# An attention and mixture-of-experts kernel: two addends move from TensorE to VectorE, one matmul group moves within a round, one product moves from GpSimd to VectorE

## The chip, the cores and the metric

One core of a Trainium2 chip runs the whole kernel in one launch. The metric is the device time of the launch in microseconds; the number to predict is the median over several runs. The engines are called by their names in the profile: PE (TensorE matmuls), PEld (its weight loads), DVE (VectorE), ACT (ScalarE), POOL (GpSimd) and SP (SyncE, here the queue that issues most transfers).

## What is computed

```python
# attention: 4 batches, 8 heads, 768 steps, head size 48
for t in range(S):
    cur   = einsum('bhd,bhe->bhde', u * k[t], v[t])
    y[t]  = einsum('bhd,bhde->bhe', r[t], state + cur)
    state = w * state + einsum('bhd,bhe->bhde', k[t], v[t])
# then, on x = y as 3072 tokens of 384 numbers:
P = exp(x @ w_gate - max);  8 rounds of: rows to sum 1, columns to sum 1, times N/E
out = sum over 8 experts of P[:, e] * (relu(x @ w1[e]) @ w2[e])     # hidden size 1024
```

All numbers are float32; the inputs and the result are in device memory.

## The kernel before, in words

The work has two stages. The attention stage (the first 207 us or so) treats the 3072 tokens as 24 tiles of 128; six tiles make one sequence, so the state starts anew at tiles 0, 6, 12 and 18. Beside it PE already computes a good part of expert 0. The expert stage (the rest) computes the other experts with a scheme of fewer products and writes the result.

The attention stage is one Python loop over rounds, `for i in range(NTT + 3)`, with i = 0 the first round; i = 11 is the twelfth. Every engine call goes through a wrapper that keeps the order in which the program was written, so **each engine executes its instructions in the order in which the loop emits them**; engines wait for each other by semaphores only. All such instructions have the wrapper's line, L30, in the profile, and are told apart by their tiles.

In round i, on PE, from i = 11 on:

- `stage_b(i+1)` transposes r and k of the next tile (`prT`, `pkT`, into PSUM); ACT copies them out as `rT` and `kT`;
- `stage_c(i)` makes the scores of tile i (`pA`, two PSUM banks, 64x64 pieces of PE); DVE copies them under the causal mask into `at`;
- `work(1)` executes one unit of expert 0: either 9 matmuls (`ph`) or 12 matmuls (`po`) of 384 columns, whose result ACT (and for `ph` DVE too) takes out;
- `state_part(i-1)` multiplies rT of the tile before with the state `S` (`py<-S,rT`, 64x64 pieces); `scores_part(i-1)` adds the product of `at` with v (`py<-vn,at`, 128x32 pieces); `state_product(i)` makes the state's increase (`py<-vn,kp`, 128x32 pieces);
- two or three more units of expert 0.

Before i = 11 the unit between `stage_c` and `state_part` is absent.

On ACT, the order around these is: the results of the units of the last round, now and then a half-precision copy of token sums (`xv<-ws`), the scaling of x (`xsc<-x,xs`, which needs DVE's `xs`), then `rT`, then `kT`. On DVE: the mask copies, a unit's low part (`hb<-ph,hb`), `x<-py,rk`, `S<-py,S`, the largest magnitude of x and its power of two (`xm` to `xs`), token sums, `kp`, the low part of x.

PSUM tiles of the tag `pa` share four buffers in turn. From i = 6 on, a round takes six: prT, pkT, pA for even and odd heads, and two for y (`y_banks`, called by `state_part` or `scores_part`, whichever comes first). So y's two banks are the buffers of that round's prT and pkT.

For the first four tiles (`tt < NE`) PE adds two addends to y by a product with the identity matrix (`addends`): the tile's `xadd` (in `hbx`, zeros in the normal case) and the bonus term `av` (in `rk`); ACT then copies y into x. From tile 4 on POOL adds `xadd` to the bonus term, and DVE adds that to y as it takes y out (`sum_x`).

`state_sum` makes the next state: DVE adds the old one (`S<-py,S`), POOL multiplies it with the decay `wbd` (`S<-S,wbd`). At the start of a sequence and for the first tiles DVE makes the product itself.

Of the kernel before, what the change touches and what calls it, by code (L numbers as in the profile page):

```python
# [13 lines left out]
ALU = mybir.AluOpType  # L14
# [19 lines left out]
def rwkv_sinkhorn_moe(  # L34
# [13 lines left out]
    V, S_, G, T, Q = (  # L48
        InOrder(tc, e) for e in (nc.vector, nc.scalar, nc.gpsimd, nc.tensor, nc.sync)
    )  # L50

    B, H, S, D = r.shape
# [6 lines left out]
    NTT = NT // P  # L59
# [10 lines left out]
    FHC = FH // P  # L70
    NPR = 15
    NE = 4

    const = ctx.enter_context(tc.tile_pool(name="const", bufs=1))
    sm = ctx.enter_context(tc.tile_pool(name="sm", bufs=2))
# [13 lines left out]
    def part(home, dtype, at, shape):  # L89

        n = 1
        for s_ in shape:
            n *= s_
        x_ = home if home.dtype == dtype else home.bitcast(dtype)
        x_ = x_[:, at : at + n]
        if len(shape) == 1:
            return x_
        names = "abcd"[: len(shape)]
        return x_.rearrange(
            f"p ({' '.join(names)}) -> p {' '.join(names)}", **{c_: s_ for c_, s_ in zip(names[1:], shape[1:])}  # L100
        )
# [14 lines left out]
    def xadd(t):  # L116
        return part(hbx, F32, t * DM, (DM,))
# [171 lines left out]
    def whole(gen):  # L289
        for _ in gen:  # L290
            pass
# [103 lines left out]
    wbd = ac.tile([P, NPAIR, D], F32, name="wbd")  # L395
# [134 lines left out]
    def prep(tt):  # L530
        ld_ = loads[tt]
        st[tt] = {}
        G.tensor_tensor(rp_[tt % 2][:, :, :D], ld_["r"], rt4, op=ALU.mult)
        if 0 < tt - 2 < NE:
            bonus(tt - 2)
        (G if 2 <= tt <= 2 * NE else V).tensor_tensor(kp_[tt % 3][:, :, :D], ld_["k"], kt4, op=ALU.mult)
        if tt == 2:
# [11 lines left out]
    def bonus(tt):  # L549
        vn = loads[tt]["v"]  # L550
        dg = at2.tile([P, H], F32, tag="dg", name=f"dg_{tt}")
        V.tensor_reduce(dg, st[tt]["rk"], axis=AX.X, op=ALU.add)
        av = st[tt].pop("rk")
        G.tensor_tensor(av, vn, dg.unsqueeze(2).broadcast_to([P, H, D]), op=ALU.mult)
        if tt >= NE:
            aq = av.rearrange("p h d -> p (h d)")
            G.tensor_tensor(aq, aq, xadd(tt), op=ALU.add)
        st[tt]["av"] = av

    def stage_b(tt):  # L560
        d = st[tt]
        for nm, src in (("rT", rp_[tt % 2]), ("kT", kp_[tt % 3])):
            pool, tag = (ps2, "po") if tt <= NE + 1 else (ps3, "pa")
            pt = pool.tile([P, NPAIR, P], F32, tag=tag, name=f"p{nm}_{tt}")
# [25 lines left out]
    def state_product(tt):  # L590
# [3 lines left out]
        kp = kp_[tt % 3].rearrange("p (a j) d -> p a (j d)", j=2)  # L594
        carry = 0 < tt < NE
        if tt:
# [11 lines left out]
    def state_sum(tt):  # L608
        d = st[tt]
        if "du" not in d:  # L610
            return
        pu = d["du"]
        sn = ss_[tt % 3]
        if tt < NE or tt % NCHB == 0:
            V.tensor_tensor(sn, pu, wbd, op=ALU.mult)
        else:
            V.tensor_tensor(sn, pu, d["S"], op=ALU.add)
            G.tensor_tensor(sn, sn, wbd, op=ALU.mult)
        st[tt + 1]["S"] = sn

    def y_banks(tt):
# [5 lines left out]
    def addends(tt):  # L627
        d = st[tt]
        d["py"] = y_banks(tt)
        for n, x_ in enumerate((xadd(tt).rearrange("p (h d) -> p h d", d=D), d["av"])):  # L630
            xg = x_.rearrange("p (a g) d -> p g a d", g=2)
            for g in range(2):
                T.matmul(d["py"][g], ident, xg[:, g], start=(n == 0), stop=False, skip_group_check=True)
        if tt + 1 < NE:
            T.matmul(d["pu"], ident, st[tt + 1]["S"], start=False, stop=False, skip_group_check=True)

    def state_part(tt):
        d = st[tt]
        if tt % NCHB == 0:
            return  # L640
        fresh = "py" not in d
        if fresh:
            d["py"] = y_banks(tt)
        for p_ in range(NPAIR):
            for g in range(2):
                rows = slice(g * HP, (g + 1) * HP)
                for hs in (slice(0, HP), slice(HP, C)):
                    T.matmul(
                        d["py"][g][hs, p_, :], d["rT"][rows, p_, hs], d["S"][rows, p_, :],
                        start=(fresh and p_ == 0), stop=False, skip_group_check=True,  # L650
                    )

    def scores_part(tt):
        d = st[tt]
        vn = loads[tt]["v"]
        at = at_[tt % 2]
        fresh = "py" not in d
        if fresh:
            d["py"] = y_banks(tt)
        for h in range(H):  # L660
            for q in range(0, P, QP):
                T.matmul(
                    d["py"][h % 2][q : q + QP, h // 2, :], at[:, h, q : q + QP], vn[:, h, :],
                    start=(fresh and h < 2), stop=(h >= H - 2), skip_group_check=True,
                )

    def sum_x(tt):
        d = st[tt]
        x = at2.tile([P, DM], F32, tag="x", name=f"x_{tt}")
        xv = x.rearrange("p (a g d) -> p g a d", g=2, d=D)  # L670
        if tt < NE:
            for g in range(2):
                S_.copy(xv[:, g], d["py"][g])
            d["x"] = x
            return
        av = d["av"].rearrange("p (a g) d -> p g a d", g=2)
        for g in range(2):
            V.tensor_tensor(xv[:, g], d["py"][g], av[:, g], op=ALU.add)
        d["x"] = x
# [148 lines left out]
    def work(n, hold=False):  # L828
        held[0] = hold
        for _ in range(n):  # L830
            if units:
                whole(units.pop(0))
        held[0] = False
# [15 lines left out]
    def run(i, place):  # L849
        for f in hooks.pop((i, place), []):  # L850
            f()
# [52 lines left out]
    for i in range(NTT + 3):  # L904
        if 1 <= i <= NE:
            stage_b(i + 1)
        run(i, "turned")
        if i + 2 < NTT and i != TH + 1:
            prep(i + 2)
        if i > NE:  # L910
            send_x(i)
        leave(0)
        if i + 1 < NTT:
            bonus_dot(i + 1)
        if NE < i < NTT - 1:
            stage_b(i + 1)
        if 1 <= i <= NE:
            addends(i - 1)
        if i <= NE:
            send_x(i)  # L920
        n = i + 5 if i < 2 else i + 4
        if i != 2 and n < NTT:
            load_part(n, "r", r)
            load_part(n, "k", k)
        if i == 0:
            load_part(3, "v", v)
        if i == 8:
            Q.dma_start(wg, w_gate.rearrange("(c p) e -> p c e", p=P))
        run(i, "loads")
        if NE <= i < NTT:  # L930
            bonus(i)
        leave(1)
        run(i, "early")
        if i < NTT:
            stage_c(i)
        if i > 10:
            work(1)
        run(i, "masked")
        if 1 <= i <= NTT:
            state_part(i - 1)  # L940
            scores_part(i - 1)
        if 2 <= i <= TH + 1:
            turn_x(i - 2)
        if i < NTT:
            state_product(i)
        if 1 <= i <= NTT:
            sum_x(i - 1)
        if i < NTT:
            state_sum(i)
        if 1 <= i <= NTT:  # L950
            bound_x(i - 1)
        if i > NTT:
            work(2)
        run(i, "middle")
        if 2 <= i < NTT - 2:
            load_part(i + 2, "v", v)
        for _ in range(n_steps(i)[0]):
            prepare()
        if i <= NTT:
            if i > TH:  # L960
                work(1 if i == 4 else 3 if i == 10 else 2, hold=i < 10)
            elif i == 0:
                S_.copy(onesb, ones)
                S_.copy(ident16, ident)
        run(i, "end")
        for _ in range(n_steps(i)[1]):
            prepare()
        if i == TH:
            prep(i + 3)
            scale_x(TH - 1)  # L970
            run(i, "last")
            units += [g1_unit(0, fc, 0) for fc in range(FHC)]
            units += [g2_half(0, t, 0, 0) for t in range(TH)]
        done = i - 2
        if TH <= done < NTT and done % TH == TH - 1:
            po_ = done // TH
            for p_, j in ((1, 0), (0, 1), (1, 1)) if po_ == 1 else ((po_, 0), (po_, 1)):
                turn[0] += 1
                g1 = [g1_unit(p_, fc, turn[0]) for fc in range(j * FHC, (j + 1) * FHC)]
                units += merged(g1, [g2_half(*a_) for a_ in pend])  # L980
                pend = [(p_, t, j, turn[0]) for t in range(TH)]
# [402 lines left out]
    for s in range(NS):  # L1384
        tasks = stage_tasks(s)
        for g in range(NG):
            for j in range(2):
                for n, nxt in enumerate(g1_slots(s, g, j)):
# [3 lines left out]
                    i = j * NPR + n  # L1392
# [37 lines left out]
```

## Time and profile before

| | |
|---|---|
| median of 3 runs | 1514.29 us (1514.22 to 1514.66) |
| the profiled execution, its own time | 1514.62 us |
| its span in the profile | 1513.1 us |
| busy: PE, DVE, ACT, POOL | 1501.1, 1010.1, 674.8, 586.8 us |
| granted PE clock | full in all slices of the span |

The span begins with the first instruction and ends with the last one; the execution's own time also holds what lies around it, 1.5 us. PE has work in 99% of the span.

### The profile page before, as it was taken

The page shows a single profiled execution, that of the slowest core. Times are in us where ns is not written, and L with a number is a line of the kernel's source. Part 1 is how long each engine was busy: PE and PEld are TensorE (multiplying, and loading weights), DVE is VectorE, ACT ScalarE, POOL GpSimd, SP SyncE. Part 2 cuts the span into 40 slices and gives each one's busy share as a digit, 9 for nine tenths or more (in the row PEclk, how much of TensorE's full clock was granted, in tenths as well). Part 3 has the DMA queues.
Part 4 walks back from the last instruction along what each step waited for, and adds up shares of the span by engine and source line. Part 5 has one row for each costly group of instructions (what it writes and reads, how often), then busy time and mean ns, then how long its engine had stood idle before and what let it go on. Part 6 is the DMA issues. An engine that isn't in the chain of part 4 may idle for free.

```text
span 1513.1 us, 28843 instructions
## 1 busy us (share of the span) xinstructions
PE 1501.1 (99%) x11654; PEld 846.7 (56%) x11656; DVE 1010.1 (67%) x1678; ACT 674.8 (45%) x1206; POOL 586.8 (39%) x687
## 2 busy tenths in 40 slices
PE   9999999999999999999999999999999999999999
PEld 7767766555555555555555555555555555555555
DVE  7998859676666666666676666666565666566464
ACT  6534425345354544445454544445353544444320
POOL 8878966200224243342425243242424233242200
PEclk9999999999999999999999999999999999999999
DMA  8965532212255576657666666655554454555434
GB/s 164 163 115 119 113 89 78 79 46 75 81 106 62 83 130 93 123 80 128 90 88 114 91 127 92 116 61 99 61 94 56 60 99 59 97 61 96 58 95 130
DMA packets 184840, 142.69 MB, mean 94 GB/s; under 512 B 107137, under 2 KB 178562, under 8 KB 184706
## 3 DMA queue, kind: packets, MB, share of 16 engines
q0 software_dynamic: 44928, 61.36, 32.6%
q1 hardware_dynamic: 139568, 79.48, 20.3%
q8 instruction: 91, 1.49, 0.4%
q14 instruction: 43, 0.35, 0.1%
q10 hardware_dynamic: 210, 0.00, 0.0%
HBM read 55.39 MB, written 80.23 MB: 90 GB/s over the span
## 4 chain that ended last, share of the span: by engine, by line
PE 95%; DVE 3%; POOL 1%; ACT 1%; issue 1%; ACTq 0%; POOLq 0%; DVEq 0%
PE po L30 49%; PE bZ L30 12%; PE bY L30 12%; PE ph L30 5%; PE bA L30 5%; PE bB L30 5%; PE py L30 2%; PE bC L30 2%; PE pA L30 1%; PE prT L30 1%; PE pkT L30 1%; POOL rk L30 0%; DVE hb L30 0%; DVE wms L30 0%; ACT hbx L30 0%
## 5 line engine op out<-in xcount | busy, mean ns | idle before, releaser
L30 PE MATMUL po<-ws,hbx 128*128 128x384 f16 x3360 | 736.8, 326 | 0.0
L30 POOL DMA_DIRECT2D accd<-stg x288 | 250.5, 870 | 694.8 <-ACT stg L30 673.9
L30 PEld LDWEIGHTS <-hbx 128*128 128x128 f16 x3360 | 328.8, 98 | 291.1
L30 PEld LDWEIGHTS <-ws 128*128 128x128 f16 x3096 | 301.0, 98 | 247.4 <-issue 3.5
L30 ACT ACTIVATE hbx<-tb 128x512 f16<-128x512 f32 x224 | 141.0, 630 | 450.8 <-DVE tb L30 450.8
L30 PE MATMUL po<-ws,hb 128*128 128x384 f16 x1248 | 323.2, 326 | 0.5 <-DVE hb L30 0.5
L30 DVE TENSOR_TENSOR tb<-bY,tb 128x512 f32<-128x512 f32 x168 | 116.2, 692 | 176.6 <-PE bY L30 175.0
L30 ACT ACTIVATE stg<-po,pe 128x384 f32<-128x384 f32 x312 | 179.1, 574 | 122.7 <-PE po L30 95.0
L30 PE MATMUL bZ<-xv,ws 128*128 128x512 f16 x840 | 227.0, 379 | 0.7 <-DVE tb L30 0.7
L30 PE MATMUL bY<-xv,ws 128*128 128x512 f16 x840 | 227.0, 379 | 0.0
L30 DVE TENSOR_TENSOR tb<-bZ,tb 128x512 f32<-128x512 f32 x168 | 115.5, 687 | 135.4 <-PE bZ L30 135.4
L30 PEld LDWEIGHTS <-hb 128*128 128x128 f16 x1248 | 121.1, 98 | 95.2 <-DVE hb L30 1.3
L30 POOL TENSOR_TENSOR ucb<-rawb 128x256 f32<-128x256 f32 x84 | 77.5, 972 | 112.7 <-DMA rawb<-in_moe_w_dram 112.7
L30 DVE TENSOR_TENSOR tb<-bB,tb 128x512 f32<-128x512 f32 x112 | 77.5, 692 | 49.2 <-PE bB L30 47.3
L30 PE MATMUL ph<-hbx,ws 128*128 128x384 f16 x576 | 104.2, 326 | 0.6 <-issue 0.3
L30 DVE SCALAR_TENSOR_TENSOR hb<-tb,hbx 128x512 f16<-128x512 f32 x112 | 77.3, 690 | 24.6 <-ACT hbx L30 19.5
L30 PE MATMUL bB<-xv,ws 128*128 128x512 f16 x336 | 90.8, 379 | 0.0
L30 PE MATMUL bA<-xv,ws 128*128 128x512 f16 x336 | 90.8, 379 | 0.0
L30 DVE SCALAR_TENSOR_TENSOR hbx<-tb,hbx 128x512 f16<-128x512 f32 x112 | 78.1, 698 | 14.7 <-ACT hbx L30 10.4
L30 ACT COPY tb<-bZ 128x512 f32<-128x512 f32 x56 | 32.8, 586 | 65.5 <-PE bZ L30 65.4
L30 ACT ACTIVATE hb<-ph 128x384 f16<-128x384 f32 x64 | 31.0, 489 | 58.6 <-PE ph L30 58.2
L30 DVE SCALAR_TENSOR_TENSOR hb<-ph,hb 128x384 f16<-128x384 f32 x64 | 34.8, 550 | 29.2 <-ACT hb L30 28.7
(181 smaller groups left out, 1492.9 us busy)
## 6 DMA issues: line engine op xcount, KB each, us to landing
accd<-stg POOLq DMA_DIRECT2D x288, 192.0 KB, 3.7
rawb<-in_moe_w_dram SPq DMA_DIRECT2D x28, 768.0 KB, 7.9
e0d<-stg SPq DMA_DIRECT2D x48, 192.0 KB, 1.9
hb<-e0d SPq DMA_DIRECT2D x48, 192.0 KB, 3.7
vn<-in_v_dram SPq DMA_DIRECT2D x24, 192.0 KB, 4.4
accd<-stg SPq DMA_DIRECT2D x24, 192.0 KB, 1.8
accd<-hb POOLq DMA_DIRECT2D x24, 192.0 KB, 4.7
rawb<-accd SPq DMA_DIRECT2D x24, 192.0 KB, 2.4
```

What stands on the lines that cost most here:

```text
L30: return lambda *a, **k: self.tc.keep_in_program_order(f(*a, **k))
```

## The change

Three edits. (1) For tiles 1 and 2, PE no longer adds `xadd`; DVE adds it while taking y out, in place of ACT's copy. (2) From i = 11 on the unit of expert 0 is no longer executed between `stage_c` and `state_part` but between `state_part` and `scores_part`. What `run(i, "masked")` emits (in rounds 11 and 12 a low part of expert 0's weights on DVE) comes ahead of the unit instead of behind it. (3) From tile 10 on DVE multiplies the state with the decay instead of POOL. In the sequence's first tiles DVE did so already, and a sequence's last tile makes no state, so this touches tiles 10, 13 to 16 and 19 to 22.

```diff
+    XV = (1, 2)
@@ state_sum
-            G.tensor_tensor(sn, sn, wbd, op=ALU.mult)
+            (V if tt > 9 else G).tensor_tensor(sn, sn, wbd, op=ALU.mult)
@@ addends
-        for n, x_ in enumerate((xadd(tt).rearrange("p (h d) -> p h d", d=D), d["av"])):
+        x_ = xadd(tt).rearrange("p (h d) -> p h d", d=D)
+        for n, x_ in enumerate([d["av"]] if tt in XV else [x_, d["av"]]):
@@ sum_x
-        if tt < NE:
+        if tt < NE and tt not in XV:
             for g in range(2):
                 S_.copy(xv[:, g], d["py"][g])
             d["x"] = x
             return
-        av = d["av"].rearrange("p (a g) d -> p g a d", g=2)
+        av = xadd(tt).rearrange("p (h d) -> p h d", d=D) if tt in XV else d["av"]
+        av = av.rearrange("p (a g) d -> p g a d", g=2)
@@ the loop over rounds
         if i < NTT:
             stage_c(i)
-        if i > 10:
-            work(1)
         run(i, "masked")
         if 1 <= i <= NTT:
             state_part(i - 1)
+        if i > 10:
+            work(1)
+        if 1 <= i <= NTT:
             scores_part(i - 1)
```

## Rows read from the trace of the kernel before

**Rows 1.** The page's chain of work that ended last, by engine.

```profile
PE 95%; DVE 3%; POOL 1%; ACT 1%; issue 1%; ACTq 0%; POOLq 0%; DVEq 0%
```

**Rows 2.** Busy time of each engine in a stretch: the rounds from i = 11 on. Columns: stretch, its length, then busy time and instructions by engine, the granted clock, DMA share and GB/s.

```profile
87.80:205.40 117.60, 116.51 (x2459) 81.30 (x2457) 103.66 (x201) 47.42 (x93) 105.06 (x110) 1.00 0.53 108
```

**Rows 3.** PE in order of time, round 2: the two addends of tile 1. Columns here and in all rows in order of time: start, length (from the first start to the last end), engine, line, operation, tiles, PE piece, shape, count, and in brackets the idle time before and what ended it.

```profile
21.58 0.81 PE L30 MATMUL py<-hbx,ident 128*128 128x192 f32 x4
22.23 0.81 PE L30 MATMUL py<-rk,ident 128*128 128x192 f32 x4
```

**Rows 4.** DVE in order of time, round 2: the state's product behind ACT's copies of x.

```profile
27.14 0.36 DVE L30 TENSOR_TENSOR S<-py,wbd 128x192 f32<-128x192 f32 x1 [1.30 <-ACT x L30]
```

**Rows 5.** All instructions that touch S or y, by form over the whole span: least, median and longest duration in ns, first and last start.

```profile
L30 DVE TENSOR_TENSOR x<-py,rk x40: 332/348/365, 44.2 to 207.3; 128x192 f32<-128x192 f32 x40
...
L30 DVE TENSOR_TENSOR S<-py,S x13: 337/346/358, 38.9 to 194.4; 128x192 f32<-128x192 f32 x13
L30 POOL TENSOR_TENSOR S<-S,wbd x13: 591/597/1311, 41.1 to 196.6; 128x192 f32<-128x192 f32 x13
```

**Rows 6.** PE in order of time, round 9, where no unit lies between pA and y.

```profile
71.43 1.10 PE L30 MATMUL pA<-rT,kT 64*64 64x128 f32 x32
72.36 0.63 PE L30 MATMUL py<-S,rT 64*64 64x48 f32 x32
72.92 0.89 PE L30 MATMUL py<-vn,at 128*32 128x48 f32 x64
73.62 0.53 PE L30 MATMUL py<-vn,kp 128*32 128x48 f32 x32
74.08 3.10 PE L30 MATMUL ph<-hbx,ws 128*128 128x384 f16 x18
```

**Rows 7.** PE in order of time, round 12, with the unit where it is before the change.

```profile
97.72 1.10 PE L30 MATMUL pA<-rT,kT 64*64 64x128 f32 x32
98.76 1.64 PE L30 MATMUL ph<-hbx,ws 128*128 128x384 f16 x9
100.33 0.68 PE L30 MATMUL py<-S,rT 64*64 64x48 f32 x32
100.94 0.89 PE L30 MATMUL py<-vn,at 128*32 128x48 f32 x64
101.64 0.50 PE L30 MATMUL py<-vn,kp 128*32 128x48 f32 x26
102.82 0.29 PE L30 MATMUL py<-vn,kp 128*32 128x48 f32 x6 [0.68 <-issue]
103.04 1.64 PE L30 MATMUL ph<-hbx,ws 128*128 128x384 f16 x9
```

**Rows 8.** PE in order of time, round 20, within the state's increase.

```profile
174.64 0.29 PE L30 MATMUL py<-vn,kp 128*32 128x48 f32 x6 [0.41 <-issue]
```

**Rows 9.** The page's DMA queues: PE's instructions (q8). Columns: packets, MB, share of the time of 16 DMA engines.

```profile
q8 instruction: 91, 1.49, 0.4%
```

**Rows 10.** PE in order of time, round 10, the last without the unit, and ACT's kT of that round.

```profile
78.63 1.10 PE L30 MATMUL pA<-rT,kT 64*64 64x128 f32 x32
80.27 0.32 PE L30 MATMUL py<-S,rT 64*64 64x48 f32 x4 [0.54 <-ACT rT L30]
80.76 0.67 PE L30 MATMUL py<-S,rT 64*64 64x48 f32 x28 [0.17 <-ACT kT L30]
81.36 0.89 PE L30 MATMUL py<-vn,at 128*32 128x48 f32 x64
...
80.10 0.61 ACT L30 COPY kT<-pkT 128x512 f32<-128x512 f32 x1
```

**Rows 11.** PE and ACT in order of time: the first and the last of the three rounds (11, 12, 22) in which ACT has no token sums to copy behind the round's last unit.

```profile
88.81 1.10 PE L30 MATMUL pA<-rT,kT 64*64 64x128 f32 x32
89.41 0.60 ACT L30 COPY kT<-pkT 128x512 f32<-128x512 f32 x1
...
188.01 1.10 PE L30 MATMUL pA<-rT,kT 64*64 64x128 f32 x32
188.61 0.60 ACT L30 COPY kT<-pkT 128x512 f32<-128x512 f32 x1
```

**Rows 12.** PE and ACT in order of time: the first and the last of the five rounds (14, 15, 16, 20, 21) in which ACT copies token sums there.

```profile
115.64 1.10 PE L30 MATMUL pA<-rT,kT 64*64 64x128 f32 x32
117.03 0.60 ACT L30 COPY kT<-pkT 128x512 f32<-128x512 f32 x1
...
179.25 1.10 PE L30 MATMUL pA<-rT,kT 64*64 64x128 f32 x32
180.57 0.60 ACT L30 COPY kT<-pkT 128x512 f32<-128x512 f32 x1
```

**Rows 13.** PE and ACT in order of time: rounds 17 and 18, in which ACT waits for DVE's xs.

```profile
143.87 1.10 PE L30 MATMUL pA<-rT,kT 64*64 64x128 f32 x32
144.24 0.62 ACT L30 ACTIVATE xsc<-x,xs 128x384 f16<-128x384 f32 x1 [0.65 <-DVE xs L30]
145.22 0.59 ACT L30 COPY kT<-pkT 128x512 f32<-128x512 f32 x1
...
152.29 1.10 PE L30 MATMUL pA<-rT,kT 64*64 64x128 f32 x32
153.77 0.59 ACT L30 COPY kT<-pkT 128x512 f32<-128x512 f32 x1
```

## The prediction, made before the changed kernel was run

> **What bounds the kernel now.** I read the chain of waits first: it runs over PE for 95% of the span [rows 1]. In such a kernel an edit is worth what it adds to or takes from PE's own line of work. So I looked next at the busy time of the stretch that edits 2 and 3 touch, the rounds from i = 11 on: PE is busy in 116.51 of 117.60 us, and behind it POOL in 105.06 and DVE in 103.66, while ACT has 47.42 [rows 2]. Nothing there lets PE make up a loss: a microsecond in which PE stands still is a microsecond at the end, and so is one saved. DVE and POOL have some 12 us to spare. The last view is each engine's work in order of time, round by round: what follows what on PE, and when ACT frees the PSUM banks that PE needs next.
>
> **Edit 1, two addends fewer on PE.** One tile's `xadd` takes PE from 21.58 to 22.23, 0.65 us [rows 3]; two tiles, 1.30 us. In exchange DVE makes four additions of about 0.35 us each [rows 5] where ACT made copies. What hides them: DVE now stands idle for 1.30 us before the next state, until ACT's copies are through [rows 4]; two additions one behind the other fit into that. If DVE were late, PE's product of the state with the identity would wait. I take a gain of 1.30; bounds 0 (the gain lost to a later wait) and 1.30.
>
> **Edit 2, PE's order.** Two things are won and one is lost.
>
> *Changes of piece.* PE's pieces are 64x64 for pA and for the state's product, 128x32 for the scores' product, 128x128 for the units. In round 9 pA is followed at once by the state's product: 0.93 us from start to start, then 0.56 to the scores' product [rows 6]. In round 12, with the unit between, pA takes 1.04, the unit 1.57, the state's product 0.61 [rows 7]. In the new order pA and the state's product stand together again: 0.93 and, if a unit is as costly to turn to as the scores' product, 0.56; the unit before the scores' product I leave at 1.57. Saved: 1.04 + 0.61 - 0.93 - 0.56 = 0.16 a round. Rounds with both pA and a state's product are 11, 12, 14 to 18 and 20 to 23, eleven: 1.76. Round 24 has no pA, so there the unit only splits two neighbours, about 0.1 lost. Net 1.65. The turn from state to unit stands in no row; were it dearer by a whole change (1.04 - 0.93 = 0.11), the gain would be 0.5. Bounds 0.5 and 1.8, and I take 1.65, since the two turns to 128x32 and to 128x128 behind pA differ little.
>
> *The gaps in the state's increase.* In round 12 the increase takes 1.40 us to the next start, with 0.68 marked as waiting for nothing that the profile shows [rows 7]; in round 9 it takes 0.46 [rows 6]. So 0.94 is lost, 0.26 more than the mark. Round 20 has a mark of 0.41 [rows 8], so about 0.67. Together 1.61. I read them as PE's instructions arriving late: 91 packets hold 1.49 MB [rows 9], 16 KB each, and the gaps come at the end of the longest run of small matmuls (32, 64 and 32 in 1.8 us). With a unit in the midst of that run, the next block has 1.6 to 2 us more to come. I take 1.3 of the 1.61, as the block borders move and one may fall badly; bounds 0 and 1.6. [...]
>
> *The new wait.* The state's product is the first to write y's two banks, and these are the buffers of the same round's prT and pkT, so it can't begin before ACT has copied rT and kT. Round 10 shows it, having no unit there: PE waits 0.54 for rT, executes 4 matmuls, waits 0.17 for kT [rows 10]. kT ends at 80.10 + 0.61 = 80.71, and the scores' product starts at 81.36, 0.65 later. Unhindered it would start 0.93 + 0.56 = 1.49 after pA, at 80.12. The loss is 1.24. From i = 11 on the unit (1.57 or more) covers this wait; the change takes the cover away. So for each round: loss = (start of kT + 0.60 + 0.65) - (start of pA + 1.49).
>
> - Rounds 11, 12, 22: ACT only has a unit's result and x's scaling before rT. 89.41 + 1.25 - 90.30 = 0.36, and 188.61 + 1.25 - 189.50 = 0.36 [rows 11]. Three rounds, 1.1.
> - Rounds 14, 15, 16, 20, 21: ACT has a copy of token sums in front as well. 117.03 + 1.25 - 117.13 = 1.15 and 180.57 + 1.25 - 180.74 = 1.08 [rows 12]. Five rounds, 5.5.
> - Rounds 17 and 18: 145.22 + 1.25 - 145.36 = 1.11 and 153.77 + 1.25 - 153.78 = 1.24, but in round 17 ACT lost 0.65 to DVE's xs [rows 13]. PE will come there later by the waits of the rounds before, which gives DVE time, while edit 3 costs it some. Between 0.36 each and 2.35 in all I take 1.1 together.
>
> ACT's chain hangs on the end of the round's last unit, as PE's does, so a wait in one round does not shorten the next one's. Rounds 13 and 19 have no state's product, 23 makes no rT and kT. Loss 1.1 + 5.5 + 1.1 = 7.7; bounds 7.3 and 9.0. Queued behind the waiting matmuls are the unit, both products of y and the round's last units, all of PE; ACT and DVE then wait for these.
>
> **Edit 3, the decay on DVE.** Nine products leave POOL, where one took 591 to 1311 ns, and come to DVE, whose nearest, the addition of the same size, takes about 346 [rows 5]. DVE gets 0.35 to 1.3 a round, bounds from these rows. The state made in round i is read in round i + 2, so neither its early nor its late end reaches PE. The product stands ahead of xm and xs, though, and xs ahead of ACT's rT. It costs nothing while the waits above give DVE more than that; without this cover it is up to 1.3 in rounds 17 and 18.
>
> **The sum.** -1.30 - 1.65 - 1.3 + 7.7 = +3.45, on the profiled execution's 1514.62: 1518.1. The median lies 0.33 below that execution, so 1517.7.
>
> **The rivals.**
>
> *The waits are paid back almost wholly.* The early rounds have gaps of the same kind as rows 8, and edit 1 removes 16 instructions ahead of them, so that every border of a block falls elsewhere. If this and edit 2 save 3.3 instead of 1.3, the sum is +1.45: 1515.7. For it: edit 2 thins the run of small matmuls. Against: before i = 11 the run stays as it is, and borders that move can fall as badly as before.
>
> *Faster.* The banks of y are free when PE comes to them: if ACT ended kT 0.4 us earlier in the three light rounds and 1.1 in the heavy ones, the loss is gone, and -4.25 is left: 1510.0. It decides as soon as the ten waits sum to under 1.2. Against it stands every round of rows 11 to 13, and round 10, where the same order did wait.
>
> [...]
>
> **How the numbers follow.** The measurement can tell about 0.2%, 3.03 us, from no change: faster is under 1511.26, slower over 1517.32. Chances: my forecast 0.55 (own range 1516.0 to 1520.0), paid back 0.30, faster 0.08, DVE 0.07. Of my forecast about 0.08 lies under 1517.32, so slower is 0.47 + 0.07 = 0.54, no change 0.30 + 0.08 = 0.38, faster 0.08. The range goes from 1513.0, which takes in most of the second case, to 1520.6, for the forecast with the waits at 9.0 and the third rival; it leaves out the faster case and thin ends.
>
> **What would show it.** Edit 1: only one pair of identity products for tiles 1 and 2, and DVE's next state no later than before. Edit 2: pA followed by `py<-S,rT` after 0.93 where nothing waits, and in ten rounds `py<-S,rT` split, 4 and 28, with idle time put down to ACT's rT and kT, about 0.36 or 1.1 us; the increase at 0.46 in all rounds from 11 on. Edit 3: no POOL product of S after tile 9, and rT not later against pA than now. The prediction is wrong if those idle times are missing or small, if the early gaps change by more than 1 us, or if a wait turns up at another place.

## The result, and the profile after

| | before | after |
|---|---|---|
| median | 1514.47 us (1513.87 to 1516.33, 6 runs) | 1521.99 us (1520.26 to 1525.88, 6 runs) |
| ratio, 95% interval | | 1.0053 [1.0043, 1.0063] |
| the profiled execution, its own time | 1514.62 us | 1525.88 us |
| its span | 1513.1 us | 1524.0 us |
| busy PE, DVE, ACT, POOL | 1501.1, 1010.1, 674.8, 586.8 us | 1505.2, 1012.8, 673.0, 577.1 us |

The change costs 7.5 us, 0.5%. The forecast was 1517.7 in a range from 1513.0 to 1520.6: slower, as forecast, but by twice as much, and 1.4 us above the range. The profiled execution is the slowest of the six, so its 10.9 us show every cause at its largest. A second profile of the same kernel is below (1520.23 us).

The first view is PE's waits from 14 to 216 us, the attention stage. Columns: who waited, the releaser, us in total, times, longest.

```profile
PE py L30 <- issue: 5.1, 4, 2.9
PE py L30 <- ACT rT L30: 3.7, 6, 1.7
PE py L30 <- ACT kT L30: 1.0, 6, 0.2
```

The second and third line were forecast: y's banks wait for ACT's copies. The first was not. It stands for time in which PE has nothing to execute and waits for nothing that the profile shows. To see where, PE in order of time, rounds 3, 6, 8 and 12:

```profile
30.66 0.28 PE L30 MATMUL py<-vn,kp 128*32 128x48 f32 x4
31.77 0.54 PE L30 MATMUL py<-vn,kp 128*32 128x48 f32 x28 [0.82 <-issue]
...
49.41 0.87 PE L30 MATMUL py<-vn,at 128*32 128x48 f32 x58
53.20 0.24 PE L30 MATMUL py<-vn,at 128*32 128x48 f32 x3 [2.92 <-issue]
...
53.75 2.39 PE L30 MATMUL ph<-hbx,ws 128*128 128x384 f16 x9
55.94 3.09 PE L30 MATMUL po<-ws,hb 128*128 128x384 f16 x12
...
69.73 0.43 PE L30 MATMUL py<-vn,kp 128*32 128x48 f32 x23
71.16 0.30 PE L30 MATMUL py<-vn,kp 128*32 128x48 f32 x9 [0.99 <-issue]
...
101.92 1.10 PE L30 MATMUL pA<-rT,kT 64*64 64x128 f32 x32
102.85 0.98 PE L30 MATMUL py<-S,rT 64*64 64x48 f32 x32
103.76 1.64 PE L30 MATMUL ph<-hbx,ws 128*128 128x384 f16 x9
105.33 0.89 PE L30 MATMUL py<-vn,at 128*32 128x48 f32 x64
106.03 0.52 PE L30 MATMUL py<-vn,kp 128*32 128x48 f32 x32
106.49 1.64 PE L30 MATMUL ph<-hbx,ws 128*128 128x384 f16 x9
```

Rounds 6 and 8 before the change:

```profile
49.72 0.78 PE L30 MATMUL py<-vn,at 128*32 128x48 f32 x50
51.46 0.33 PE L30 MATMUL py<-vn,at 128*32 128x48 f32 x11 [0.96 <-issue]
...
66.54 0.35 PE L30 MATMUL py<-vn,kp 128*32 128x48 f32 x15
67.22 0.38 PE L30 MATMUL py<-vn,kp 128*32 128x48 f32 x17 [0.33 <-issue]
```

Before, round 6 had such a gap of 0.96 us, with 50 of the 64 scores' matmuls done; now it comes after 58 and lasts 2.92. In round 8 it came after 15 of 32 and lasted 0.33; now after 23, and 0.99. Both lie exactly 8 matmuls later. Edit 1 removed 8 matmuls, with their 8 weight loads 16 instructions, so the gaps stay at the same place in the stream of instructions and move in the work. They sit on the borders of blocks: the page counts 11646 matmuls and 11648 weight loads on PE and 91 packets of its instructions, so about 256 in a packet. Behind the gap of round 6 the unit ph takes 2.39 us and po 3.09, where they take 1.64 and 2.12 elsewhere. That is the clock: in the window below (columns as in [rows 2]) it is granted at 0.70 on average, and at 0.50 from 54.50 to 57.50 us.

```profile
53.20:58.90 5.70, 5.70 (x60) 3.21 (x61) 4.01 (x10) 0.99 (x2) 4.70 (x6) 0.70 0.76 119
...
119.00:127.00 8.00, 6.14 (x110) 3.65 (x112) 6.12 (x8) 3.53 (x9) 7.76 (x9) 0.79 0.50 100
```

Round 12 at the end of the list is edit 2 as forecast. The state's product starts 0.93 behind pA, its 0.98 instead of the 0.63 of [rows 6] holds the wait for ACT, and the increase takes 0.46 to the next start (106.03 to 106.49) without the gap of [rows 7].

The second window is round 14. PE, DVE and ACT there, in order of time:

```profile
119.09 1.10 PE L30 MATMUL pA<-rT,kT 64*64 64x128 f32 x32
121.88 0.32 PE L30 MATMUL py<-S,rT 64*64 64x48 f32 x4 [1.69 <-ACT rT L30]
122.37 0.80 PE L30 MATMUL py<-S,rT 64*64 64x48 f32 x28 [0.17 <-ACT kT L30]
123.10 3.61 PE L30 MATMUL po<-ws,hb 128*128 128x384 f16 x12
...
115.82 1.20 DVE L30 TENSOR_TENSOR S<-S,wbd 128x192 f32<-128x192 f32 x1
...
118.53 0.16 DVE L30 RECIPROCAL swg<-iswg 128x1 f32<-128x1 f32 x1
...
118.79 0.31 ACT L30 ACTIVATE wgp<-wg,swg 128x24 f16<-128x24 f32 x1 [4.66 <-DVE swg L30]
...
119.26 0.47 ACT L30 COPY stg<-po 128x384 f32<-128x384 f32 x1
119.63 0.49 ACT L30 ACTIVATE hb<-ph 128x384 f16<-128x384 f32 x1
120.01 0.83 ACT L30 CAST xv<-ws 128x768 f16<-128x768 f32 x1
120.73 0.62 ACT L30 ACTIVATE xsc<-x,xs 128x384 f16<-128x384 f32 x1
121.25 0.58 ACT L30 COPY rT<-prT 128x512 f32<-128x512 f32 x1
```

Read it backwards. PE waits 1.69 us for rT. ACT works without a pause from 118.79 to rT, and began only then because it waited for `swg`, the scale of the gate's weights, which DVE makes in this round alone. DVE was late because the decay product, new on it by edit 3, took 1.20 us ahead of that. Behind the wait PE's unit po takes 3.61 instead of 2.12 us, at a granted clock of 0.50 from 123 to 126 us.

The round-by-round sums agree with this. Measured from pA to pA, the profiled execution loses 4.00 us against before up to round 11, 6.82 from there to round 23, and 0.10 behind it; together 10.92, the difference of the spans. Of the 4.00, edit 1 gives −0.65 ahead of pA in rounds 2 and 3 each, and the steps with the gaps of rounds 3, 6 and 8 cost +1.10, +3.51 and +0.66. Round 3's share is no matter of the moved border: the same step is longer than in this profile of before in all the other thirteen of this case, by 0.40 to 1.73, with the borders put back too. Of the 6.82, round 14 alone has 3.86.

### The profile page after: what moved, and what is told of

Read it like the earlier page. It is cut to its first block, busy times and chain, and to the rows that moved or that the text cites. A ratio compares the mean times of both kernels' runs of the same rounds, so it can differ in the third digit from the quotient of the medians.

```text
span 1524.0 us, 28828 instructions
## 1 busy us (share of the span) xinstructions
PE 1505.2 (99%) x11646; PEld 848.6 (56%) x11648; DVE 1012.8 (66%) x1691; ACT 673.0 (44%) x1202; POOL 577.1 (38%) x678
## 4 chain that ended last, share of the span: by engine, by line
PE 90%; POOL 3%; DVE 3%; ACT 2%; issue 2%; DMA 1%; SPq 0%; ACTq 0%; POOLq 0%; DVEq 0%
PE po L30 47%; PE bZ L30 12%; PE bY L30 12%; PE bA L30 5%; PE bB L30 5%; PE ph L30 4%; PE bC L30 2%; PE py L30 2%; POOL rk L30 1%; POOL ws L30 1%; POOL rp L30 1%; PE pA L30 0%; DMA vn<-in_v_dram 0%; DVE hb L30 0%; ACT hb L30 0%
## 5 line engine op out<-in xcount | busy, mean ns | idle before, releaser
L30 DVE TENSOR_TENSOR tb<-bB,tb 128x512 f32<-128x512 f32 x112 | 77.4, 691 | 49.1 <-PE bB L30 47.2
```

Of the source, the lines that this page charges most:

```text
L30: return lambda *a, **k: self.tc.keep_in_program_order(f(*a, **k))
```

## The experiments

**Theories.** A: the forecast's waits behind edit 2 are the main loss, and edit 1's removed instructions lengthen the early gaps by moving the borders of the instruction blocks. B, a rival: edit 3 makes DVE the bound. C, a rival: edit 1's extra additions make DVE late in the early rounds, and the gaps have nothing to do with it. Runs of one group share a chip and its runs of before.

### One edit at a time (before on this chip: 1514.44 us)

Edit 1 alone (`XV`, `addends` and `sum_x` as in the change):

> Edit 1 alone (tiles 1 and 2 without xadd on PE). Theory, the moved borders: the 16 PE instructions that are gone ahead of round 3 move every border of a 256-instruction block in the small matmuls of rounds 3 to 10, and PE stands longer there, by about 5.4 us in the changed kernel's profile (gaps marked as waiting for nothing of 0.82, 0.22, 2.92, 0.99 and 0.32 against 0.34, 0.96 and 0.33 before). Then this edit alone makes the kernel slower: -1.3 + 5.4 = about +4, and the profile shows the gap of about 3 us within py<-vn,at of round 6. Rival, the sum of my prediction: the gaps belong to the new order or to one execution, and this edit alone gives -1.3.

Edit 2 alone:

```diff
         if i < NTT:
             stage_c(i)
-        if i > 10:
-            work(1)
         run(i, "masked")
         if 1 <= i <= NTT:
             state_part(i - 1)
+        if i > 10:
+            work(1)
+        if 1 <= i <= NTT:
             scores_part(i - 1)
```

> Edit 2 alone (the unit between the state's product and the scores' product). The borders up to round 10 are where they were before the change. Theory, the waits for ACT's rT and kT: about +7.7 - 1.65 - 1.3 = +4.7, the waits split 4 and 28 matmuls in ten rounds, the early gaps as before (0.34, 0.96, 0.33). Rival, the parting costs what the whole change costs: +7.5 and more, with the long gap of round 6 present here as well.

Edit 3 alone (the one line of `state_sum`):

> Edit 3 alone (DVE multiplies the state with the decay from tile 10 on). Theory: nothing, within 1 us, because without edit 2 the unit of 1.6 to 2 us between pA and the state's product covers ACT's lateness; in round 14 ACT's rT comes about 0.9 us later against pA than before, because DVE's chain to the gate's weights is that much later. Rival, DVE as the bound: slower by 2 us or more, with PE waiting for ACT or DVE in rounds 13 to 22.

All three edits, and 16 PE instructions (8 small warm-up matmuls with their weight loads) added ahead of the first tile, so that the blocks' borders behind round 3 fall where they did before:

```diff
-    def spin(n):
+    def spin(n, cols=TB):
...
-            T.matmul(pz, zeros[:, :P], zeros, start=True, stop=True)
+            T.matmul(pz[:, :cols], zeros[:, :P], zeros[:, :cols], start=True, stop=True)
...
-    spin(4)
+    spin(12, 168)
```

> All three edits, and 8 matmuls more in the warm-up on zeros (12 of 168 columns in place of 4 of 512, the same work), so that PE has as many instructions ahead of round 3's borders as before the change. Theory, the moved borders: the early gaps are as before the change (0.34, 0.96, 0.33), and the time falls from +7.5 to between +2 and +4. Rival: the gaps come from the work that left PE or from DVE's additions, the gap of about 3 us in round 6 stays, and the time stays at +7.5.

| kernel | median, us | against before | ratio [95%] |
|---|---|---|---|
| edit 1 | 1515.60 | +1.2 | 1.0009 [1.0000, 1.0018] |
| edit 2 | 1519.02 | +4.6 | 1.0031 [1.0019, 1.0044] |
| edit 3 | 1514.84 | +0.4 | 1.0004 [0.9995, 1.0013] |
| all three and fill | 1519.95 | +5.5 | 1.0039 [1.0025, 1.0053] |

Edit 1, which takes 1.3 us of work from PE, makes the kernel no faster; if anything, slower, though by less than the +4 that was expected. Its profile shows the 0.65 saved twice, and gaps of 0.83, 1.66 and 1.46 us in rounds 3, 6 and 8, after the same counts of matmuls as in the changed kernel; the late gaps of rounds 12 and 20 are gone. Edit 2 costs what was forecast for it (7.7 − 1.65 − 1.3 = 4.75); only five of the ten waits that were expected to be split in 4 and 28 are marked so, those of the table below. Edit 3 alone costs nothing that can be measured, which speaks against B; in its round 14 rT starts 1.2 us later against pA (0.9 was expected), and the unit covers it. The fill takes 2 us off, less than expected: +5.5 lies above the +2 to +4 named for it. Its profile has the gap of round 6 back after 50 matmuls with 0.96 us, but 0.90 instead of 0.33 in round 8 and 1.42 in round 3, where the profile of before has none. PE's waits for ACT with edit 2 alone, rounds 14, 15 and 16, 20, 21:

| round | 14 | 15 | 16 | 20 | 21 |
|---|---|---|---|---|---|
| wait for rT, edit 2 alone, us | 0.45 | 0.39 | 0.31 | 0.43 | 0.38 |
| the changed kernel | 1.69 | 0.38 | 0.31 | 0.43 | 0.38 |

Only round 14 differs, and only when edit 3 is there.

### The changed kernel again, and parts of it with the fill (before: 1513.96 us)

The changed kernel, unaltered:

> The changed kernel once more, beside the others of this call on one chip. Both theories: +6.5 to +8.5 against the kernel before, of which +1.2, +4.6 and +0.4 are what the three edits gave alone.

Edit 1 with the fill:

> Edit 1 alone, with the 8 extra warm-up matmuls that put the borders of the instruction blocks back. Theory, the moved borders: what edit 1 lost comes back, -1.3 against the kernel before and about -2.5 against edit 1 without them (which gave +1.2). Rival, the loss lies in DVE's four additions or in the later rounds: +1, as without them.

Edits 1 and 2 with the fill, the decay left on POOL:

> Edits 1 and 2 with the borders put back, without edit 3: the kernel of 12 shorter matmuls in the warm-up, with the decay on POOL again. With all three edits it gave +5.5. Theory, DVE's product delays ACT in round 14 (through the gate's weights) and the wait for rT there grows by 0.4 to 0.9 us: +3.4 to +4.6 here, the first wait of round 14 back at about 0.45 us. Rival, the decay on DVE costs nothing: +5.5.

The same, and from round 5 on ACT scales x behind the copies rT and kT instead of ahead of them:

```diff
-        if i > NE:
-            send_x(i)
...
         if NE < i < NTT - 1:
             stage_b(i + 1)
+        if i > NE:
+            send_x(i)
```

> As the last one, and ACT copies rT and kT out before it scales x instead of behind it (from round 5 on). Theory, ACT's lateness is what edit 2 loses: kT ends 0.52 us earlier against pA, the waits of the light rounds vanish and those of the heavy ones halve to about 0.55, so 3.5 to 4.5 us come back: -1 to +1 against the kernel before. Rival, the loss is in the new order itself (changes of piece that the sum got wrong) or ACT's later x makes PE wait elsewhere: the time stays at +3 or more.

| kernel | median, us | against before | ratio [95%] |
|---|---|---|---|
| changed kernel | 1521.28 | +7.3 | 1.0054 [1.0040, 1.0067] |
| edit 1 and fill | 1513.45 | −0.5 | 0.9998 [0.9989, 1.0007] |
| edits 1, 2 and fill | 1518.99 | +5.0 | 1.0031 [1.0019, 1.0043] |
| and ACT's copies first | 1517.23 | +3.3 | 1.0022 [1.0013, 1.0031] |

Edit 1 with the fill was expected at −1.3, its rival at +1; −0.5 lies between, and its interval holds no change.

The second profile of the changed kernel has gaps of 0.56, 1.83 and 1.27 us in rounds 3, 6 and 8, at the same places as the first, and 0.89 of wait in round 14. The two units behind the gap of round 6 take 1.64 and 2.11 us, the one behind the wait 2.12, and its time is 5.65 us under the first's. So the places are fixed by the program and the lengths vary from one execution to the next.

Edits 1 and 2 with the fill show the same from the other side: there the border of round 6 is back after 50 matmuls, and the profiled execution (1521.70, the slowest of its six) has a gap of 2.88 us at it and 2.82 for the 9 matmuls behind. So a long gap can come at the old place too.

Without edit 3 the wait of round 14 is back at 0.45 (1.03 for the round, against 1.46 with edit 3 and the fill). The medians can't tell this: +5.0 lies above the +3.4 to +4.6 that was expected, and its interval holds the rival's +5.5. The traces do. In the first profile of the changed kernel DVE's product of round 14 took 1.20 us, ACT waited 4.66 for `swg` and PE 1.69 for rT; in the second profile, and in that of all three edits with the fill, it is 0.40, 3.86 and 0.89; without edit 3 there is no product, and ACT waits 3.42 and PE 0.45. So the coupling goes by way of `swg`. Its price is about 0.4 us where the product takes 0.40, and 1.2 us of wait where it takes 1.20, with the granted clock of 0.50 behind it.

With ACT's copies first, the loss of rounds 11 to 23 falls from 3.92 to 0.45 in the profiles, as theory A wants: the waits are ACT's lateness. The time improves by less (1.8 us, to +3.3, where −1 to +1 was expected and the rival said +3 or more). In the early rounds of its profile the late x makes a new wait: DVE waits 1.14 us for ACT's `xsc` in round 5, PE then stands 2.52 us for DVE's `hb` in round 6, and the 9 matmuls behind it take 2.96 us instead of 1.64.

### Edit 1 once more, and a kernel that keeps the gain (before: 1514.37 us)

Edits 1 and 2 with the fill, the decay on POOL, `send_x` behind the copies from round 11 on only, and the token sums' steps at the first of their two places in a round:

```diff
-        return (0, 0) if i < 10 else (2, 2) if i < 21 else (3, 2)
+        return (0, 0) if i < 10 else (4, 0) if i < 21 else (5, 0)
...
-        if i > NE:
+        if NE < i <= 10:
             send_x(i)
...
+        if i > 10:
+            send_x(i)
```

> Edits 1 and 2 with the borders put back and the decay on POOL; from round 11 on ACT copies rT and kT out before it scales x, and from round 10 on all token-sum steps come ahead of the round's last units, so that ACT's copies of token sums are done while PE is in those units. Theory, ACT's lateness is all that edit 2 loses: the waits for rT and kT are gone except in round 14 (gate's weights), rounds 11 to 23 take 2 to 3 us less than before the change, and the whole is -2 to -4. Rival, the token sums ahead of the units make a unit's result leave late and PE waits for that instead: 0 or slower.

Edit 1 alone, again:

> Edit 1 alone again, on one chip with the next. Theory, the moved borders: +1 against the kernel before, 1.5 to 2.5 us above the next.

Edit 1 with the fill, again:

> Edit 1 alone with the borders put back, again. Theory, the moved borders: -0.5 to -1.3 against the kernel before. Rival: the same as edit 1 without the extra matmuls, within 0.7 us.

The kernel before with the fill, so that the borders fall 8 matmuls earlier than before:

> The kernel before with the 8 extra warm-up matmuls alone: every border comes 8 matmuls earlier in the work. Theory, the moved borders: the gap in py<-vn,at of round 6 comes after 42 of 64 matmuls instead of 50, those in py<-vn,kp of rounds 8, 12 and 20 after 7 and 18 instead of 15 and 26, and the time moves by some tenths to 2 us either way. Rival: gaps stay where they are in the work, and the time is that of the kernel before.

| kernel | median, us | against before | ratio [95%] |
|---|---|---|---|
| edits 1, 2, fill, ACT in time | 1512.67 | −1.7 | 0.9989 [0.9980, 0.9998] |
| edit 1 | 1514.97 | +0.6 | 1.0006 [0.9997, 1.0015] |
| edit 1 and fill | 1513.55 | −0.8 | 0.9996 [0.9987, 1.0005] |
| before and fill | 1514.77 | +0.4 | 1.0001 [0.9992, 1.0010] |

The eleven executions of edit 1 alone fall into two groups: six from 1513.49 to 1514.97 and five from 1516.87 to 1518.41. In the first try two of eleven lie above 1516.8 as well, 1518.06 and 1518.23. With the fill none of the 22 executions of the two tries does (the longest took 1516.49), and of before one of 33 on this chip (1517.56). The profiled execution of edit 1, 1517.55, is of the upper group. PE in its round 6:

```profile
49.00 0.87 PE L30 MATMUL py<-vn,at 128*32 128x48 f32 x58
53.54 0.24 PE L30 MATMUL py<-vn,at 128*32 128x48 f32 x3 [3.68 <-issue]
...
54.10 3.01 PE L30 MATMUL ph<-hbx,ws 128*128 128x384 f16 x9
56.91 2.46 PE L30 MATMUL po<-ws,hb 128*128 128x384 f16 x12
```

The gap is 3.68 us, and the two units behind it take 1.72 us more than their 1.64 and 2.11 (3.01 + 2.46 − 3.75), with the clock down again (granted 0.76 on average from 51 to 58 us). With the fill the same round reads:

```profile
49.01 0.89 PE L30 MATMUL py<-vn,at 128*32 128x48 f32 x64
49.72 0.52 PE L30 MATMUL py<-vn,kp 128*32 128x48 f32 x32
51.31 1.62 PE L30 MATMUL ph<-hbx,ws 128*128 128x384 f16 x9 [1.07 <-DVE hb L30]
...
55.30 0.34 PE L30 MATMUL po<-ws,hb 128*128 128x384 f16 x1 [0.58 <-DVE hb L30]
```

No gap, but 1.07 and 0.58 us for DVE's `hb`, which the gap had covered. Part of theory C holds here: DVE sets the pace of these rounds. It does so without edit 1 too (edit 3 alone shows 0.17 and 0.57 of the same waits, edit 2 alone 0.24). Busy times of the engines in rounds 3 to 7, before the change and with edit 1 and the fill (columns as in [rows 2]):

```profile
33.50:64.30 30.80, 29.45 (x702) 22.05 (x701) 30.15 (x60) 18.15 (x31) 30.09 (x29) 1.00 0.92 173
...
33.50:64.30 30.80, 29.07 (x704) 21.96 (x707) 30.00 (x60) 18.23 (x31) 30.09 (x29) 1.00 0.98 172
```

Between DVE's instructions (30.15 and 30.00 us) there is no idle time over 0.04 us in this stretch. POOL is nearly as full (30.09 us each time); no run separates the two. DVE's instruction for the state of round 3 starts at 33.10 before and at 32.94 here, so its additions do not make it late. PE's pA of round 8 starts at 64.35 and 64.16. In the six profiles with edit 1 and no stop of over 2 us it starts at 64.03 to 64.22; without edit 1 at 64.20 (edit 2 alone), 64.35 (before), 64.68 (before and fill) and 65.12 (edit 3 alone). So of the 1.30 us that PE saves in rounds 2 and 3, between nothing and about 1 us is left at round 8, by the profile that is compared.

The fill on the kernel before was to put gaps after 42, 7 and 18 matmuls. In part it did: round 8 has one after 7 (0.15 us, below what the view marks). In round 6 there is none after 42; instead the gap in the two units ahead of it, 0.34 us after 13 of 18 matmuls before, is 1.36 us after 5. Rounds 12 and 20 have none. The time did not change (+0.4 us, with an interval that holds no change): here the moved borders fell harmlessly.

All profiles but that of before with the fill, by where the border lies. A dash is a round without a marked gap:

| gap, us | profiles | mean |
|---|---|---|
| round 3, with edit 1 (four without fill; six with) | 0.82, 0.56, 0.83, 0.66; 1.42, 0.94, 0.87, 1.33, 0.94, 0.87 | 0.92 |
| round 3, without edit 1 (before; edit 2; edit 3) | –; 0.28; 0.93 | 0.40 |
| round 6, after 58 (edit 1, no fill) | 2.92, 1.83, 1.66, 3.68 | 2.52 |
| round 6, after 50 (before; edit 2; edit 3; six with fill) | 0.96; 0.96; 0.52; 0.96, –, –, 2.88, –, 0.40 | 0.74 |
| round 8, after 23 | 0.99, 1.27, 1.46, 1.63 | 1.34 |
| round 8, after 15 | 0.33; 0.89; 0.48; 0.90, –, 0.88, –, –, 0.52 | 0.44 |

In rounds 6 and 8 the gap at the border that edit 1 moves is some 1.8 and 0.9 us longer on average; in round 3 the place of the border makes no such difference. Round 6's gap of 1.66 or 1.83 costs nothing by round 8 (pA there at 64.22 and 64.03), because PE would have waited for DVE; those of 2.92 and 3.68 put that pA at 67.54 and 67.89. Round 8's gap is paid: that step is 1.13 longer than before with 1.46 us of gap, against 0.33. On the other side edit 1 ends the late gaps: rounds 12 and 20 get 0.94 and 0.68 shorter with it alone.

The pair edit 1 with and without the fill, on one chip, differs by 1.4 us in the medians (1.5 to 2.5 was expected), in the direction that A wants, but the two intervals overlap. In the other two comparisons the fill is worth 1.7 us (edit 1, +1.2 to −0.5) and 1.8 (all three, +7.3 to +5.5), each across two chips. Three differences of one sign, the 7 executions of 22 above 1516.8 against none, and the traces make the case; no one difference of medians alone does.

Edits 1 and 2 with ACT in time have the lowest median of all, 0.9 us under edit 1 with the fill, and an interval just below that of no change; −1.7 is a little short of the −2 to −4 that was expected. PE in round 17 there, and ACT's copies:

```profile
143.18 1.10 PE L30 MATMUL pA<-rT,kT 64*64 64x128 f32 x32
144.11 0.63 PE L30 MATMUL py<-S,rT 64*64 64x48 f32 x32
144.67 1.64 PE L30 MATMUL ph<-hbx,ws 128*128 128x384 f16 x9
...
142.85 0.59 ACT L30 COPY rT<-prT 128x512 f32<-128x512 f32 x1
143.34 0.60 ACT L30 COPY kT<-pkT 128x512 f32<-128x512 f32 x1
143.81 0.63 ACT L30 ACTIVATE xsc<-x,xs 128x384 f16<-128x384 f32 x1
```

0.93 and 0.56 from start to start, as the forecast had it for an unhindered round. kT starts 0.16 behind pA's start; before, it started 1.35 behind [rows 13]. Only round 14 still waits (0.39 and 0.17). Rounds 11 to 23 are 2.15 us shorter than before in the profile.

## Why the prediction was right in its direction and wrong in its size

**Edit 2, pieces: right.** The forecast was 0.16 a round. The profile of edit 2 alone gives, from pA to pA, +0.20 in rounds 11 and 22, which is 0.36 − 0.16.

**Edit 2, the late gaps: right, a little low.** Round 12 changed by −0.75, which is 0.36 − 0.16 − 0.94 to a hundredth. Both late gaps went, so the term is 1.61 and not the 1.3 taken. In the changed kernel this gain is not edit 2's alone, since edit 1 by itself ends both gaps as well. That the gaps are late instructions is now more than a reading. A fill of 16 instructions moves or removes them and touches nothing that PE waits for. And the trace holds PE's instruction packets one by one: all 44 gaps marked "issue" in rounds 3 to 20 of the 14 profiles end 1.24 to 1.62 us after the end of a packet, always the same packet for the same border.

**Edit 2, the new wait: right.** The heavy rounds 14, 15, 16 and 21 gave +1.05, +0.91, +0.86 and +0.93, where 1.1 − 0.16 = 0.94 was forecast. Rounds 17 and 18 gave 0.20 and 0.13, so about 0.65 of wait together (with 0.16 each) instead of 1.1: DVE was given time, as argued, and they became light rounds. In that profile rounds 11 to 23 and the end behind them sum to +3.74, a microsecond under the forecast's 4.75 by the gaps (0.31), rounds 17 and 18 (0.45) and small parts; the median of its runs is +4.6, with an interval from 2.9 to 6.7 that holds both.

**Edit 3: right alone, wrong together.** Alone it costs nothing measurable. The product on DVE takes what the bounds said, 0.35 to 1.3. Forms of S in the changed kernel, columns as in [rows 5]:

```profile
L30 DVE TENSOR_TENSOR S<-py,S x13: 345/348/357, 38.7 to 204.4; 128x192 f32<-128x192 f32 x13
L30 DVE TENSOR_TENSOR S<-S,wbd x9: 357/776/1197, 88.9 to 204.8; 128x192 f32<-128x192 f32 x9
```

The two are of one size and differ in where their inputs lie; the sum with an input in PSUM never exceeds 357 ns, also in the seven of thirteen that a POOL instruction overlaps. Of the nine products with both in SBUF, the five of 0.78 us and more all begin while a POOL instruction is under way, and the three with no POOL instruction beside them take 0.36; the ninth, at 175.89, has POOL instructions beside it and takes 0.36 too. The trace shows no more than this of what makes five of them long. But DVE did not become the bound, since only one of ten waits grew. The forecast's 0.07 for that, and the third rival that its range takes in, stand for a product of 1.3 us each time, which no run shows: in the changed kernel four of the nine took 0.36 us and five 0.78 to 1.20. The failed sentence is "It costs nothing while the waits above give DVE more than that". I named rounds 17 and 18 as the ones without cover, because ACT waited for xs there. I did not look at what else ACT waits for from DVE. In round 14 it is `swg`, and the same row stands in the trace of before (ACT waited 3.41 us for it there, until 114.10). The price is 0.4 us where the product is short, by the two profiles with the fill.

**Edit 1: wrong, and the step that failed.** The term was −1.30 with bounds from 0 to −1.30. The local price was exact, 0.65 in rounds 2 and 3 each. The term measured +0.6 and +1.2 in two tries, and −0.5 and −0.8 where the fill puts the borders back. Two things failed in it.

First, the saving does not last. By the sentence "an edit is worth what it adds to or takes from PE's own line of work" it should, but PE waits behind it. At the border of round 3 the packet of instructions that PE needs ends at 29.98 to 30.57 us in thirteen of the fourteen profiles (31.32 with edit 3 alone), with edit 1 or without. PE comes there up to 1.3 us earlier with edit 1 and stands longer, 0.56 to 1.42 us against at most 0.28, or 0.93 with edit 3 alone. Behind that DVE works without a pause up to round 8 where no long stop comes (no idle time over 0.04 us in the two windows above). The bound of 0, "the gain lost to a later wait", named such a loss, but the sum took the whole 1.30, and the busy times that I had read were those from i = 11 on. What the fill shows as −0.5 and −0.8 is not the 1.30 either: its two profiles are at −0.47 and +0.35 up to round 11, and rounds 11 to 23 are 1.26 and 1.35 us shorter, since most of the late gaps is gone there too.

Second, the borders. The prediction knew of them ("every border of a block falls elsewhere"), put them into a rival as a gain, and wrote "borders that move can fall as badly as before" only as the reason against that gain. The sign that it named, early gaps that change by more than 1 us, came: round 6 went from 0.96 to 2.92. It had the means to do better: the borders lie about 256 instructions apart, so the new places (after 58 matmuls in round 6, after 23 in round 8) could have been counted beforehand. What could not be read from that trace is the length: at one place it was 1.66 to 3.68 us in four executions, and the trace of before showed 0.96 at most. But its gaps of rows 7 and 8 and those of the early rounds were the nearest rows, and a bound on the side of loss, of a microsecond or two, was owed where I put 0.

**The sum.** The single edits measure +1.2, +4.6 and +0.4: 6.2, against 7.3 and 7.5 for all three. But edit 1 and edit 2 each end the late gaps, so this sum counts 1.6 us of gain twice. With that and the 0.4 of round 14 it is 8.2, or 7.6 with the second try of edit 1. The intervals are wider than the difference to 7.3 and 7.5, and no run separates it further.

**What stays open.** Why a gap at one place is 1.7 us in one execution and 3.7 in the next is half answered. The packet that ends round 6's gap starts at 46.0 to 46.5 us in the three profiles with the fill that have no gap, at 48.3 to 49.1 where the gap is 0.52 to 1.83, and at 50.7 to 51.1 where it is 2.88 to 3.68. So the gap is long where the packet is late. Why it starts late is not shown. The transfers are dense there (the DMA share is over 0.9 for most of 46 to 53 us), but no run varied them, and nothing shows that they delay the packet. That the fill's gain is by the gaps alone rests on the traces, not on a separated measurement.

## What to carry to other kernels

An instruction that is removed from a long program is worth its time only if no other engine sets the pace behind it, and if the borders of the instruction blocks behind it fall no worse: here 1.30 us taken from PE measured +1.2 and +0.6, and −0.5 and −0.8 with the borders put back. So look at the busy times of the very rounds behind the edit; and where PE executes many short matmuls in a row, count the place of every "issue" gap in instructions and move it by what is removed (8 matmuls here). A unit that stands between a producer and its consumer is cover (here 1.57 us or more from start to start, without which PE waited 0.31 to 0.45 us for rT in the five rounds of the table): before it is moved, compare the copy that frees the bank with the new start, round by round, and reorder the copying engine first. When an operation goes to another engine, look at everything which that engine releases in each round, also what happens in one round only, as with `swg` here (0.89 and 1.69 us of wait in place of 0.45).

## What the runs showed of the hardware that was not expected

A gap in PE's instructions cost twice in two of the profiles. After 2.92 and 3.68 us in round 6, the next 21 matmuls of 384 columns took 1.72 us longer than elsewhere, at a granted clock of 0.70 and 0.76 on the average of the windows above (in the first, 0.50 from 54.50 to 57.50 us). With ACT's copies first, the 9 matmuls behind a wait of 2.52 us for DVE took 2.96 instead of 1.64 us. After 1.66 and 1.83 us in the same place as the long gaps the units took 1.64 and 2.11 us, as elsewhere, but in round 14 the granted clock was 0.50 behind a wait of 1.69. So the length of the stop alone does not tell these cases apart.

The gaps at the borders of blocks of about 256 instructions were 0.2 to 3.7 us long where they are marked. PE resumed 1.24 to 1.62 us after the end of the block's packet. In the expert stage no such gap is marked in the big products: from 216 us on, PE's waits in the changed kernel are one of 0.9 us for DVE's `tb` and one of 0.5 for its `hb`. In the attention stage the marked gaps lie mostly in or beside runs of short matmuls, but also in a unit of 384 columns (0.34, 0.67 and 1.36 us in round 5 of three profiles).
